# A separate pair of buffers for the last output group, and smaller first loads, in a fused attention + gMLP kernel

## Chip, cores, metric

The kernel runs on one core of one Trainium2 chip. The metric is device time in microseconds (us) of one execution, lower is better. Every quoted time is the median of several executions; a profile is of one execution, and its span (first to last instruction) is 1.7 to 1.9 us shorter than that execution's time. A run is called slow when it is over 1.5% above the fastest of its kernel; such runs are left out of the ratios, and where a median contains one, the table says so.

## Reference

A layer norm feeds a sliding-window attention (32 heads of 16, window 8, dilation 2) and a gated MLP with a spatial product. Both results are added to x. In short, with S = 2048 and D = 512 in bf16:

```python
xn = layernorm(x)                                  # [2048, 512]
q, k, v = split(xn @ wqkv)                         # wqkv [512, 1536]
attn = softmax(q . k at offsets 0,2,..,14) . v
z  = gelu(xn @ w_in)                               # [2048, 1376], halves z1, z2
g  = w_sp @ layernorm(z2) + b_sp                   # w_sp [2048, 2048]
out = x + attn @ wo + (z1 * g) @ w_out
```

## The kernel before

The work is planned by hand: every engine has a fixed order of instructions, TensorE is nearly always busy, and tiles of 128 tokens are grouped as four blocks j of four tiles tb. Only the two ends matter here.

**Start.** The first block's tiles ("x tiles 1 to 4") are loaded first: tiles 1 and 2 in halves on two issuing engines, tiles 3 and 4 in one transfer of 256 KB on ScalarE's queue. SyncE loads the query weights (512 KB, "first weights"), the second x block (512 KB) and the key weights (512 KB).

```python
def load_wqk(E, s):                                # s=0 query weights, s=1 key weights
    E.dma_start(wqk[:, s],
                A_wqkv[:, s * D:(s + 1) * D].rearrange("(k p) f -> p k f", p=P))

for tb in range(2):
    load_x0(SP, tb, 0)
    load_x0(A, tb, 1)
A.dma_start(xall[:, 0, 2:4, :], xblk[0][:, 2:4, :])
load_wqk(SP, 0)
SP.dma_start(xall[:, 1], xblk[1])
load_wqk(SP, 1)
for j in range(2, 4):
    SP.dma_start(xall[:, j], xblk[j])
SP.dma_start(w_z2[:], ...)
# ... cut: constants, layer norm helpers
pqs = [qk_tile() for _ in range(3)]
qk_part(pqs[0], 0, 0, 0, 2, kcs=range(2))          # query products of tiles 1, 2
qk_part(pqs[0], 0, 0, 0, 2, kcs=range(2, 4))
tr_copy(t0[2], tr(t0[2]))                          # transpose tile 3 on TensorE
qk_part(pqs[1], 0, 1, 0, 2, (0,))
tr_copy(t0[3], tr(t0[3]))                          # transpose tile 4
qk_part(pqs[1], 0, 1, 0, 2, (1,))
qk_part(pqs[0], 0, 0, 2, 3)                        # query products of tile 3: 16 matmuls of 128 columns
qk_part(pqs[1], 0, 1, 2, 3)
qk_part(pqs[2], 0, 2, 0, 2)                        # first key products: need the key weights
# ... cut
for n in range(2):
    qk_part(pqs[n], 0, n, 3, 4)                    # query products of tile 4
    qk_copy(pqs[n], 0, n)
```

VectorE takes each tile's statistics (`ln_stats`), ScalarE a square root, VectorE normalises the tile, TensorE transposes it. The statistics of tile 4 stand in VectorE's order ahead of tile 3's normalisation, so tile 3's transposition needs both tiles.

**End.** The output has four groups o of four tiles. Each tile's sum waits in PSUM; VectorE adds x to it (`out_add`) and SyncE or ScalarE stores the result. All four groups share four x buffers `xr_t` and four result buffers `ot_t`, which lie in the dead part of the q/k region:

```python
xr_t = [r_qk[:, QE + 4096 + n * D:QE + 4096 + (n + 1) * D] for n in range(4)]
ot_t = [r_qk[:, QE + 6144 + n * D:QE + 6144 + (n + 1) * D] for n in range(4)]

def load_xr(o):
    for tb in range(TB):
        i = 4 * tb + ORD[o]
        SP.dma_start(xr_t[tb], x2[i * P:(i + 1) * P, :])

def out_add(o, tb, part=0):
    pc, cs = tiles["o", o][tb][part]
    V.tensor_tensor(ot_t[tb][:, cs], pc, xr_t[tb][:, cs], ALU.add)

def out_store(o, tb, part=0, E=SP):
    i = 4 * tb + ORD[o]
    pc, cs = tiles["o", o][tb][part]
    E.dma_start(out2[i * P:(i + 1) * P, cs], ot_t[tb][:, cs])
```

So an addition of the last group may not overwrite a result buffer before the previous group's store from it has landed. `r_pr`, the region of the attention products, is free by then.

Of the kernel before, what the change touches and what calls it, by code (L numbers as in the profile page):

```python
# [11 lines left out]
ALU = mybir.AluOpType  # L12
# [3 lines left out]
P = 128  # L16
S = 2048
D = 512
NT = S // P
TB = 4  # L20
TBS = 512
C = D // P
# [48 lines left out]
def kernel(  # L71
# [13 lines left out]
    V = nc.vector  # L85
    A = nc.scalar
    G = nc.gpsimd
    PE = nc.tensor
    SP = nc.sync

    x2 = A_x.rearrange("b s d -> (b s) d")
    out2 = out.rearrange("b s d -> (b s) d")
    xblk = x2.rearrange("(b j p) d -> j p b d", b=TB, j=4)
# [9 lines left out]
    xall = r_x[:, 0:4 * TB * D].rearrange("p (j b d) -> p j b d", j=4, b=TB)  # L103
    vp = r_x[:].rearrange("p (d t) -> p d t", d=DH)
    r_w = sb.tile([P, 8192], BF16, name="r_w")
    wqk = r_w[:, 0:4096].rearrange("p (s k f) -> p s k f", s=2, k=C)
# [9 lines left out]
    xr_t = [r_qk[:, QE + 4096 + n * D:QE + 4096 + (n + 1) * D] for n in range(4)]  # L116
    ot_t = [r_qk[:, QE + 6144 + n * D:QE + 6144 + (n + 1) * D] for n in range(4)]
# [8 lines left out]
    r_pr = sb.tile([P, 2 * 4 * C * TB * P], BF16, name="r_pr")  # L126
# [2 lines left out]
    uT = r_uz[:, NZ1 * FPAD:].rearrange("p (s m t) -> p s m t", s=2, m=MCH)  # L129
    pr_home = [r_pr[:, 0:8192], r_pr[:, 8192:16384], r_uz[:, (NZ1 + 8) * FPAD - 8192:]]  # L130
    pr = [h.rearrange("p (c w b t) -> p c w b t", w=4, c=C, b=TB) for h in pr_home]
    pw_t = [r_pr[:, n * 2048:(n + 1) * 2048].rearrange("p (d t) -> p d t", d=DH) for n in range(4)]
    op = r_pr[:, 8192:16384].rearrange("p (d t) -> p d t", d=DH)

# [29 lines left out]
    def load_x0(E, tb, h):  # L164
        E.dma_start(xall[:, 0, tb, 256 * h:256 * h + 256], x2[tb * TBS:tb * TBS + P, 256 * h:256 * h + 256])  # L165

    def load_wqk(E, s):
        E.dma_start(wqk[:, s],
                    A_wqkv[:, s * D:(s + 1) * D].rearrange("(k p) f -> p k f", p=P))

    for tb in range(2):
        load_x0(SP, tb, 0)
        load_x0(A, tb, 1)
    A.dma_start(xall[:, 0, 2:4, :], xblk[0][:, 2:4, :])
    load_wqk(SP, 0)
    SP.dma_start(xall[:, 1], xblk[1])
    load_wqk(SP, 1)
    for j in range(2, 4):
        SP.dma_start(xall[:, j], xblk[j])
    SP.dma_start(w_z2[:], B_w_in[:, FH:F].rearrange("(k p) f -> p k f", p=P))  # L180
# [121 lines left out]
    def qk_part(pq, j, m, b0, b1, ccs=(0, 1), p0=None, kcs=range(C)):  # L302
        sd, c0 = m // 2, 2 * (m % 2)
        p0 = b0 if p0 is None else p0
        xv = xnT[:].rearrange("p k (b j t) -> p k b j t", b=TB, j=4)
        for cc in ccs:
            for kc in kcs:
                PE.matmul(pq[:, cc, p0 * P:(p0 + b1 - b0) * P], wqk[:, sd, kc, c0 + cc:D:C],  # L308
                          xv[:, kc, b0:b1, j, :], start=(kc == 0), stop=(kc == C - 1))

    def qk_copy(pq, j, m, b0=0, b1=TB, p0=None):
        sd, c0 = m // 2, 2 * (m % 2)
        p0 = b0 if p0 is None else p0
        if sd == 0:
            dst = qs[:, j, c0:c0 + 2, b0 * P:b1 * P].rearrange("p c (b t) -> p c b t", b=b1 - b0)
        else:
            dst = ks[:, c0:c0 + 2, HALO:HALO + S].rearrange("p c (b j t) -> p c b j t", b=TB, j=4)[:, :, b0:b1, j, :]
        cast = A.copy(dst, pq[:, :, p0 * P:(p0 + b1 - b0) * P].rearrange("p c (b t) -> p c b t", b=b1 - b0))  # L318
        if sd == 1:
            for i in k_reads[j]:  # L320
                tc.declare_no_dep(cast.ins, i, reason="other token columns of the same rows")
            k_casts[j].append(cast.ins)

    def qk_tile():
        return ps_mm.tile([P, 2, TBS], F32, name="pq", tag="mm")
# [147 lines left out]
    def load_xr(o):  # L473
        for tb in range(TB):
            i = 4 * tb + ORD[o]
            SP.dma_start(xr_t[tb], x2[i * P:(i + 1) * P, :])  # L476

    def out_heads(o):
        last = o == 3
# [30 lines left out]

    def out_add(o, tb, part=0):
        pc, cs = tiles["o", o][tb][part]
        V.tensor_tensor(ot_t[tb][:, cs], pc, xr_t[tb][:, cs], ALU.add)  # L513

    def out_store(o, tb, part=0, E=SP):
        i = 4 * tb + ORD[o]
        pc, cs = tiles["o", o][tb][part]
        E.dma_start(out2[i * P:(i + 1) * P, cs], ot_t[tb][:, cs])

    def out_full(o, tb, part=0):  # L520
        pc, cs = tiles["o", o][tb][part]
# [9 lines left out]
    def last_adds():  # L531
        for tb, part, E in ((2, 0, SP), (3, 0, A), (3, 1, SP)):
            out_add(3, tb, part)
            out_store(3, tb, part, E)
# [41 lines left out]
    pqs = [qk_tile() for _ in range(3)]  # L576
# [3 lines left out]
    qk_part(pqs[1], 0, 1, 0, 2, (0,))  # L580
    tr_copy(t0[3], tr(t0[3]))
    qk_part(pqs[1], 0, 1, 0, 2, (1,))
    qk_part(pqs[0], 0, 0, 2, 3)
    qk_part(pqs[1], 0, 1, 2, 3)
    qk_part(pqs[2], 0, 2, 0, 2)
    for n in range(2):
        ln_stats(i1[n])
# [4 lines left out]
    ln_apply(i1[1])  # L592
    ln_stats(i1[3])
    for n in range(2):
        qk_part(pqs[n], 0, n, 3, 4)
        qk_copy(pqs[n], 0, n)
    ln_sqrt(slice(9, 16, 4))
    ln_stats(i2[0])
# [22 lines left out]
    pqs = [qk_tile() for _ in range(3)]  # L621
# [32 lines left out]
    def halo_zero():  # L654
# [9 lines left out]
             "M": sm_max, "E": sm_exp, "S": lambda h, k: sm_sum(h, k), "R": sm_norm, "mask": add_mask,  # L664
             "G": g_mm, "Gi": g_bias, "U": u_mul, "T": u_tr, "A": lambda k: ap[k](),
             "O": out_heads, "Or": out_rest, "Oh": out_half, "F": out_add, "s": out_store, "end": last_adds,
             "halo": halo_zero, "wo": load_wo, "late": load_late, "xr": load_xr, "w": load_wsp}
    for tok in ORDER.split():
        name = tok.rstrip("0123456789.")
# [31 lines left out]
```

## Time and profile before

| | before |
|---|---|
| time, median of 3 runs | 203.91 us (203.90 to 204.33) |
| the profiled execution | 204.95 us, span 203.2 us |
| TensorE busy | 97% of the span |
| start: VectorE waits for x tiles 3 and 4 | 0.87 us |
| end: last addition starts after TensorE's end | 0.66 us |

From the page of the profile before: its head, the busy times, and the chain of waits that ended last, as shares of the span.

```profile
span 203.2 us, 4070 instructions
PE 196.3 (97%) x1687; PEld 124.8 (61%) x1691; DVE 187.2 (92%) x267; ACT 100.1 (49%) x162; POOL 11.2 (6%) x14
...
PE 89%; DMA 4%; DVE 2%; SPq 2%; issue 1%; ACTq 0%; DVEq 0%
```

PE is TensorE, PEld its weight loads, DVE VectorE, ACT ScalarE, SPq and ACTq the issuing of transfers. The chain is TensorE but for some microseconds, and those lie at the ends.

The timeline of before at the start. Columns: start in us, duration, engine, line, operation, output<-input, shapes, count, and in brackets the idle time ahead of it and what ended it.

```profile
1.72 0.43 SPq L168 DMA_DIRECT2D r_w<-in_A_wqkv_dram  x1
1.73 0.46 ACTq L174 DMA_DIRECT2D r_x<-in_A_x_dram  x1
...
2.19 0.51 SPq L176 DMA_DIRECT2D r_x<-in_A_x_dram  x1
...
2.74 0.51 SPq L168 DMA_DIRECT2D r_w<-in_A_wqkv_dram  x1
...
5.57 0.41 DVE L216 TENSOR_SCALAR r_x<-r_x,mv,rstd 128x512 bf16<-128x512 bf16 x1
...
6.85 0.69 DVE L205 BATCH_NORM_STATS2 stats<-r_x 128x6 f32<-128x512 bf16 x1 [0.87 <-DMA r_x<-in_A_x_dram]
...
9.11 0.40 PE L223 MATMUL pt<-ident,r_x 128*128 128x128 bf16 x4 [1.18 <-DVE r_x L216]
```

VectorE has tile 2 normalised at 5.98 and then waits 0.87 us for tile 3, whose load was issued at 1.73. TensorE pays for it at 9.11, with the transposition of tile 3. The other lines are the issues of the first weights (1.72), the second x block (2.19) and the key weights (2.74).

The timeline of before at the end:

```profile
196.52 4.62 SPq L518 DMA_DIRECT2D out_dram<-r_qk  x6
...
197.61 0.69 DVE L513 TENSOR_TENSOR r_qk<-po,r_qk 128x512 bf16<-128x512 f32 x1 [5.02 <-PE po L523]
198.83 0.69 DVE L513 TENSOR_TENSOR r_qk<-po,r_qk 128x512 bf16<-128x512 f32 x1 [0.53 <-DMA out_dram<-r_qk]
199.10 0.64 PE L523 MATMUL pb<-r_w,r_uz 128*128 128x224 bf16 x5
199.44 1.05 DVE L513 TENSOR_TENSOR r_qk<-pa,r_qk 128x512 bf16<-128x512 f32 x2
200.40 0.38 DVE L513 TENSOR_TENSOR r_qk<-pb,r_qk 128x224 bf16<-128x224 f32 x1
```

The second addition waits 0.53 us for a store (the previous group's, from the same result buffer). TensorE ends at 199.10 + 0.64 = 199.74, and the last addition begins only at 200.40.

### The profile page before, as it was taken

How to read it: one execution, taken by the hardware profiler on the slowest of the kernel's cores; microseconds unless marked ns; L12 is line 12 of the kernel's file. 1: busy time of each engine (PE TensorE's matmuls, PEld its weight loads, DVE VectorE, ACT ScalarE, POOL GpSimd, SP SyncE). 2: the span in 40 equal slices, each digit the busy share in tenths (PEclk: the TensorE clock that was granted, in tenths of full speed). 3: DMA queues.
4: the chain of work that ended last, by engine and by line, in shares of the span. 5: the costliest groups of instructions: out<-in, count | busy, mean ns of one | idle time of the engine just before them, and what ended most of it. 6: DMA issues, size and time to landing. Idle time of an engine off the chain costs nothing.

```text
span 203.2 us, 4070 instructions
## 1 busy us (share of the span) xinstructions
PE 196.3 (97%) x1687; PEld 124.8 (61%) x1691; DVE 187.2 (92%) x267; ACT 100.1 (49%) x162; POOL 11.2 (6%) x14
## 2 busy tenths in 40 slices
PE   7699999999999999999999999999999999999993
PEld 2499866565566666666556666666546645664561
DVE  5789899999999999999989998999999999999714
ACT  3566999999969984641742309546100210131000
POOL 3000000592000000000000000000000000000000
PEclk9999999999999999999999999999999999999999
DMA  4972548200298000695699957997927910743253
GB/s 151 357 253 53 101 99 177 76 0 3 55 185 176 3 0 0 120 257 113 29 212 198 215 155 103 209 175 148 194 40 196 222 26 14 212 110 93 51 185 130
DMA packets 66290, 25.91 MB, mean 127 GB/s; under 512 B 56224, under 2 KB 66016, under 8 KB 66016
## 3 DMA queue, kind: packets, MB, share of 16 engines
q1 hardware_dynamic: 65568, 25.19, 54.7%
q10 hardware_dynamic: 704, 0.47, 0.7%
q8 instruction: 13, 0.21, 0.5%
q14 instruction: 5, 0.04, 0.1%
HBM read 10.13 MB, written 2.10 MB: 60 GB/s over the span
## 4 chain that ended last, share of the span: by engine, by line
PE 89%; DMA 4%; DVE 2%; SPq 2%; issue 1%; ACTq 0%; DVEq 0%
PE pg L451 37%; PE pz L237 18%; PE pq L308 13%; PE pv L412 7%; PE po L523 6%; PE po L499 5%; DMA r_x<-in_A_x_dram 3%; SPq L476 1%; DVE r_qk L513 1%; PE pl L362 1%; DMA out_dram<-r_qk 1%; PE po L508 1%; DVE stats L205 1%; PE pt L223 1%; ACTq L165 0%
## 5 line engine op out<-in xcount | busy, mean ns | idle before, releaser
L451 PE MATMUL pg<-z,r_qk 128*128 128x344 bf16 x448 | 67.3, 309 | 0.0
L451 PEld LDWEIGHTS <-r_qk 128*128 128x128 bf16 x448 | 43.7, 98 | 22.4 <-issue 0.8
L237 PE MATMUL pz<-w_z,xnT 128*128 128x344 bf16 x256 | 40.1, 309 | 0.0
L426 DVE TENSOR_TENSOR r_pr<-r_x,r_w 128x2048 bf16<-128x2048 bf16 x32 | 38.2, 1217 | 0.3
L430 DVE TENSOR_TENSOR r_pr<-r_pr 128x2048 bf16<-128x2048 bf16 x28 | 33.8, 1217 | 0.2
L457 ACT ACTIVATE gs<-pg,b_col 128x688 bf16<-128x688 f32 x16 | 13.3, 832 | 40.6 <-PE pg L451 25.1
L237 PEld LDWEIGHTS <-xnT 128*128 128x128 bf16 x256 | 24.9, 98 | 13.4 <-issue 0.8
L308 PE MATMUL pq<-xnT,r_w 128*128 128x256 bf16 (+2 forms) x192 | 28.7, 303 | 0.1
L342 DVE TENSOR_TENSOR r_pr<-r_qk 128x2048 bf16<-128x2048 bf16 x24 | 28.4, 1216 | 0.0
L308 PEld LDWEIGHTS <-r_w 128*128 128x128 bf16 x200 | 20.3, 114 | 7.1 <-DMA r_w<-in_A_wqkv_dram 0.4
L299 ACT ACTIVATE r_uz<-pz 128x688 bf16<-128x688 f32 x16 | 11.5, 742 | 22.5 <-PE pz L237 22.3
L318 ACT CAST r_qk<-pq 128x1024 bf16<-128x1024 f32 (+1 forms) x16 | 15.3, 990 | 2.4 <-PE pq L308 2.3
L523 PE MATMUL po<-r_w,r_uz 128*128 128x512 bf16 x66 | 14.9, 379 | 0.6 <-issue 0.6
L513 DVE TENSOR_TENSOR r_qk<-po,r_qk 128x512 bf16<-128x512 f32 x14 | 9.2, 684 | 6.5 <-PE po L523 6.0
L412 PE MATMUL pv<-xnT,r_w 128*32 128x512 bf16 x256 | 14.6, 380 | 0.0
L499 PE MATMUL po<-r_lg,r_pr 32*128 32x512 bf16 x224 | 14.5, 375 | 0.0
L523 PEld LDWEIGHTS <-r_uz 128*128 128x128 bf16 x85 | 8.0, 98 | 9.7 <-issue 1.5
L351 DVE TENSOR_TENSOR r_pr<-r_pr 128x4096 bf16<-128x4096 bf16 x6 | 13.7, 2281 | 0.0
L205 DVE BATCH_NORM_STATS2 stats<-r_x 128x6 f32<-128x512 bf16 (+1 forms) x18 | 10.9, 615 | 2.1 <-DMA r_x<-in_A_x_dram 2.1
L261 ACT ACTIVATE junk<-z 128x688 bf16<-128x688 bf16 x16 | 12.5, 778 | 0.2
L412 PEld LDWEIGHTS <-r_w 128*32 128x32 bf16 x256 | 9.5, 138 | 4.5 <-issue 0.3
L255 ACT ACTIVATE z<-pz 128x688 bf16<-128x688 f32 x16 | 11.8, 739 | 0.8 <-PE pz L237 0.8
(81 smaller groups left out, 174.6 us busy)
## 6 DMA issues: line engine op xcount, KB each, us to landing
r_lg<-in_A_wo_dram SPq DMA_DIRECT2D x8, 256.0 KB, 4.2
r_qk<-in_A_x_dram SPq DMA_DIRECT2D x16, 128.0 KB, 2.4
out_dram<-r_qk SPq DMA_DIRECT2D x15, 128.0 KB, 2.1
r_w<-in_A_wqkv_dram SPq DMA_DIRECT2D x3, 512.0 KB, 5.2
r_x<-in_A_x_dram SPq DMA_DIRECT2D x3, 512.0 KB, 6.0
w_z<-in_B_w_in_dram SPq DMA_DIRECT2D x2, 688.0 KB, 5.6
r_w<-in_B_w_out_dram SPq DMA_DIRECT2D x1, 640.0 KB, 5.0
r_x<-in_A_x_dram ACTq DMA_DIRECT2D x1, 256.0 KB, 5.1
```

The lines of the kernel that those rows point to most:

```text
L237: PE.matmul(pz[:, hh, 0:FHALF], xnT[:, kc, i * P:(i + 1) * P], wz[:, kc, hh * FHALF:(hh + 1) * FHALF], start=(kc == 0), stop=(kc == C - 1))
L308: PE.matmul(pq[:, cc, p0 * P:(p0 + b1 - b0) * P], wqk[:, sd, kc, c0 + cc:D:C], xv[:, kc, b0:b1, j, :], start=(kc == 0), stop=(kc == C - 1))
L318: cast = A.copy(dst, pq[:, :, p0 * P:(p0 + b1 - b0) * P].rearrange("p c (b t) -> p c b t", b=b1 - b0))
L342: prod = V.tensor_tensor(pr[g % 3][:, c].rearrange("p w b t -> p b w t"), q3.unsqueeze(2).broadcast_to([P, TB, 4, P]), k4, ALU.mult)
L351: V.tensor_tensor(pr[g % 3][:, 0:2], pr[g % 3][:, 0:2], pr[g % 3][:, 2:4], ALU.add)
L412: PE.matmul(pv[32 * tb:32 * tb + 32, dd, :], wv[:, kc, 2 * d2 + dd, :], xnT[:, kc, tb * TBS:(tb + 1) * TBS], start=(kc == 0), stop=(kc == ...
L426: V.tensor_tensor(pw_t[n], vp[:, :, off:off + P], a_sb[:, slot_w(w), ts].unsqueeze(1).broadcast_to([P, DH, P]), ALU.mult)
L430: V.tensor_tensor(pw_t[n] if dst is None else dst, pw_t[n], pw_t[m], ALU.add)
L451: PE.matmul(pg[:, hh, 0:FHALF], wsp[n][:, k, :], z2[:, k, hh * FHALF:(hh + 1) * FHALF], start=(k == 0), stop=(k == NT - 1))
L457: A.activation(gs[:], tiles.pop(("g", n))[:, :, 0:FHALF], ACT.Identity, bias=b_col[:, i:i + 1])
L499: PE.matmul(pc, op[32 * tb:32 * tb + 32, d, o * P:(o + 1) * P], wo_r[32 * tb:32 * tb + 32, d, cs], start=(d == 8), stop=False, tile_positi ...
L523: PE.matmul(pc, uT[:, o % 2, m, tb * P:(tb + 1) * P], wout[:, m, cs], start=False, stop=(m == MCH - 3))
```

## The change

Its intent has two parts. At the end, the last group gets its own x and result buffers in the free products' region, so that no addition waits for a store. At the start, x tiles 3 and 4, the first weights and the second x block each come in two transfers, so that the first halves land sooner; the key weights go ahead of the second half of the x block; and the query products of tiles 3 and 4 are computed together in matmuls of 256 columns, which also moves tile 3's behind the first key products. The order in which the rest of the kernel's steps are queued is the same. This is the whole diff:

```diff
--- before.py
+++ after.py
@@ -129,6 +129,8 @@
     uT = r_uz[:, NZ1 * FPAD:].rearrange("p (s m t) -> p s m t", s=2, m=MCH)
     pr_home = [r_pr[:, 0:8192], r_pr[:, 8192:16384], r_uz[:, (NZ1 + 8) * FPAD - 8192:]]
     pr = [h.rearrange("p (c w b t) -> p c w b t", w=4, c=C, b=TB) for h in pr_home]
+    xl_t = [r_pr[:, n * D:(n + 1) * D] for n in range(4)]
+    ol_t = [r_pr[:, (4 + n) * D:(5 + n) * D] for n in range(4)]
     pw_t = [r_pr[:, n * 2048:(n + 1) * 2048].rearrange("p (d t) -> p d t", d=DH) for n in range(4)]
     op = r_pr[:, 8192:16384].rearrange("p (d t) -> p d t", d=DH)
 
@@ -164,17 +166,20 @@
     def load_x0(E, tb, h):
         E.dma_start(xall[:, 0, tb, 256 * h:256 * h + 256], x2[tb * TBS:tb * TBS + P, 256 * h:256 * h + 256])
 
-    def load_wqk(E, s):
-        E.dma_start(wqk[:, s],
-                    A_wqkv[:, s * D:(s + 1) * D].rearrange("(k p) f -> p k f", p=P))
+    def load_wqk(E, s, k0=0, k1=C):
+        E.dma_start(wqk[:, s, k0:k1],
+                    A_wqkv[:, s * D:(s + 1) * D].rearrange("(k p) f -> p k f", p=P)[:, k0:k1])
 
     for tb in range(2):
         load_x0(SP, tb, 0)
         load_x0(A, tb, 1)
-    A.dma_start(xall[:, 0, 2:4, :], xblk[0][:, 2:4, :])
-    load_wqk(SP, 0)
-    SP.dma_start(xall[:, 1], xblk[1])
+    for tb in range(2, TB):
+        A.dma_start(xall[:, 0, tb], xblk[0][:, tb])
+    load_wqk(SP, 0, 0, 2)
+    load_wqk(SP, 0, 2, 4)
+    SP.dma_start(xall[:, 1, 0:2], xblk[1][:, 0:2])
     load_wqk(SP, 1)
+    SP.dma_start(xall[:, 1, 2:4], xblk[1][:, 2:4])
     for j in range(2, 4):
         SP.dma_start(xall[:, j], xblk[j])
     SP.dma_start(w_z2[:], B_w_in[:, FH:F].rearrange("(k p) f -> p k f", p=P))
@@ -473,7 +478,7 @@
     def load_xr(o):
         for tb in range(TB):
             i = 4 * tb + ORD[o]
-            SP.dma_start(xr_t[tb], x2[i * P:(i + 1) * P, :])
+            SP.dma_start((xl_t if o == 3 else xr_t)[tb], x2[i * P:(i + 1) * P, :])
 
     def out_heads(o):
         last = o == 3
@@ -510,12 +515,13 @@
 
     def out_add(o, tb, part=0):
         pc, cs = tiles["o", o][tb][part]
-        V.tensor_tensor(ot_t[tb][:, cs], pc, xr_t[tb][:, cs], ALU.add)
+        xr, ot = (xl_t, ol_t) if o == 3 else (xr_t, ot_t)
+        V.tensor_tensor(ot[tb][:, cs], pc, xr[tb][:, cs], ALU.add)
 
     def out_store(o, tb, part=0, E=SP):
         i = 4 * tb + ORD[o]
         pc, cs = tiles["o", o][tb][part]
-        E.dma_start(out2[i * P:(i + 1) * P, cs], ot_t[tb][:, cs])
+        E.dma_start(out2[i * P:(i + 1) * P, cs], (ol_t if o == 3 else ot_t)[tb][:, cs])
 
     def out_full(o, tb, part=0):
         pc, cs = tiles["o", o][tb][part]
@@ -580,8 +586,6 @@
     qk_part(pqs[1], 0, 1, 0, 2, (0,))
     tr_copy(t0[3], tr(t0[3]))
     qk_part(pqs[1], 0, 1, 0, 2, (1,))
-    qk_part(pqs[0], 0, 0, 2, 3)
-    qk_part(pqs[1], 0, 1, 2, 3)
     qk_part(pqs[2], 0, 2, 0, 2)
     for n in range(2):
         ln_stats(i1[n])
@@ -592,7 +596,7 @@
     ln_apply(i1[1])
     ln_stats(i1[3])
     for n in range(2):
-        qk_part(pqs[n], 0, n, 3, 4)
+        qk_part(pqs[n], 0, n, 2, 4)
         qk_copy(pqs[n], 0, n)
     ln_sqrt(slice(9, 16, 4))
     ln_stats(i2[0])
```

## Prediction

> **What bounds the kernel now.** The chain of waits is 89% TensorE, and the table of waits shows TensorE waiting only at the two ends; between 9.11 us and 199.7 us it has no gap above 0.2 us. VectorE is busy 92%, but nothing there waits for it. So only start and end can give time.
>
> *Start.* The timeline shows VectorE free at 5.98 us (second tile normalised) and starting the third tile's statistics at 6.85: 0.87 us of waiting for the 256 KB load of x tiles 3 and 4 (landed 5.1 us after issue). The rest follows at a fixed distance: root, normalisation 8.64, transposition 9.11, before which TensorE idled 1.18 us. The first weight matrix (512 KB) landed at the same time. From 4 us the DMA engines run full at about 360 GB/s. The Trainium skill ("DMA: Bandwidth & Descriptors", section "Issuing engines are not separate DMA queues") says that queues interleave on the same 16 engines; the common landing at 6.8 us agrees.
>
> *End.* TensorE ends at 199.74. VectorE's last additions should follow it, but the second starts at 198.83, 0.53 us after the first ended, "released by DMA out": it overwrites a result buffer whose store was issued at 196.52 and landed at 198.75. The third (199.44) waits likewise. The last addition starts at 200.40, 0.66 us behind TensorE.
>
> **What the change does.**
> 1. x tiles 3 and 4 come as two 128 KB transfers, the weights as two 256 KB ones. My estimate, from cumulated GB/s of the windows (768 KB of both queues landed at 6.75; half of it is moved about 1 us earlier): tile 3 and the first weight half land at 5.4 to 5.9, before VectorE is free; tile 4 at 6.2 to 6.8, needed at 6.8. Gain: the full 0.87 us, at most 0.3 less; all engines shift together.
> 2. The key weights go ahead of half of the second x block: landed (estimate) at about 9, needed at about 9.6, as TensorE reaches them 1.7 us earlier. In the compiled program each transfer waits for the eighth before it, so later loads are issued 0.5 to 1 us later; a backlog of 768 KB hides that.
> 3. 32 matmuls of 128 columns (56 ns each in the chain) become 16 of 256 (109 ns): nothing.
> 4. The last group reads x and writes results in the products' buffers, free since 188.7. Queue order there is unchanged; x lands at 196.8 to 198.5, early enough. Additions start at 197.61, 198.22, 198.83, 199.44, 199.80 (spacing from the trace): 0.60 us gained, all on the chain to the last store.
>
> Sum: 0.85 + 0.6 = 1.45 us; I take off 0.05: **202.5 us, 202.1 to 203.3** eight times in ten. Faster by over 2%: 1%; within 2%: 98%; slower: 1%.
>
> **What would show it.** Right: third tile's statistics at about 6.0 and its transposition at about 8.25; TensorE idle before it 0.3 us; no gap later; last addition within 0.15 us of the last matmul; no wait for a store in the last group. Wrong: statistics still waiting for x after 6.3; TensorE waiting for key weights near 9.6; an addition waiting for x; TensorE gaps later that give the gain back.
>
> **What would make it wrong.** Smaller transfers landing no earlier, since the engines drain everything together (203.3); late key weights; the first x load of the last group, whose issue took 1.57 us, arriving late (up to 0.5 us). A gain above 1.5 us I see no source for.

## Result and the profile after

A ratio here is the mean time of one kernel's fast runs over the mean of the other's of the same rounds, so it is not quite the ratio of the medians.

| | before | after | ratio, 95% interval |
|---|---|---|---|
| median of 4 runs each, same chip | 204.12 (203.9 to 204.7) | 203.77 (203.56 to 203.85) | 0.9977 (0.9953 to 1.0001) |
| profiled execution: time | 204.95 | 203.85 | |
| profiled execution: span | 203.2 | 202.0 | |

Within 2%, as was held likely; but the predicted 1.4 us became 0.35 in the medians, outside the range of 202.1 to 203.3. The two profiles differ by 1.2 us, nearly what was predicted. Profiles and times do not tell the same story, and that is the first thing to explain.

The page of after: head, busy times, chain.

```profile
span 202.0 us, 4038 instructions
PE 196.5 (97%) x1671; PEld 124.7 (62%) x1675; DVE 187.1 (93%) x267; ACT 100.0 (50%) x162; POOL 11.5 (6%) x14
...
PE 90%; DMA 3%; DVE 2%; SPq 2%; ACTq 1%; issue 1%; DVEq 0%
```

Timeline of after, start:

```profile
1.72 0.95 SPq L170 DMA_DIRECT2D r_w<-in_A_wqkv_dram  x2
1.73 0.96 ACTq L177 DMA_DIRECT2D r_x<-in_A_x_dram  x2
...
3.14 0.37 SPq L180 DMA_DIRECT2D r_x<-in_A_x_dram  x1
...
3.55 0.47 SPq L170 DMA_DIRECT2D r_w<-in_A_wqkv_dram  x1
...
5.71 0.68 DVE L210 BATCH_NORM_STATS2 stats<-r_x 128x6 f32<-128x512 bf16 x1
...
6.79 0.69 DVE L210 BATCH_NORM_STATS2 stats<-r_x 128x6 f32<-128x512 bf16 x1 [0.18 <-DMA r_x<-in_A_x_dram]
...
8.26 0.40 PE L228 MATMUL pt<-ident,r_x 128*128 128x128 bf16 x4 [0.51 <-DVE r_x L221]
...
9.74 2.98 PEld L313 LDWEIGHTS <-r_w 128*128 128x128 bf16 x28 [0.26 <-DMA r_w<-in_A_wqkv_dram]
```

Tile 3 no longer makes VectorE wait, tile 4 by 0.18 us, and TensorE transposes tile 3 at 8.26 instead of 9.11. But the key weights are issued at 3.55 instead of 2.74, and TensorE's weight loads wait for them at 9.74, which they did not before.

Timeline of after, end:

```profile
196.91 1.29 DVE L519 TENSOR_TENSOR r_pr<-po,r_pr 128x512 bf16<-128x512 f32 x2 [5.02 <-PE po L529]
...
198.11 1.04 DVE L519 TENSOR_TENSOR r_pr<-pa,r_pr 128x512 bf16<-128x512 f32 x2
198.40 0.64 PE L529 MATMUL pb<-r_w,r_uz 128*128 128x224 bf16 x5
199.08 0.39 DVE L519 TENSOR_TENSOR r_pr<-pb,r_pr 128x224 bf16<-128x224 f32 x1
```

No addition waits for a store. The last one begins 0.04 us after TensorE's end at 199.04.

### The profile page after: what moved, and what is told of

It reads as the page before. It is cut to its first block, busy times and chain, and to the rows that moved or that the text cites. A ratio compares the mean times of both kernels' runs of the same rounds, so it can differ in the third digit from the quotient of the medians.

```text
span 202.0 us, 4038 instructions
## 1 busy us (share of the span) xinstructions
PE 196.5 (97%) x1671; PEld 124.7 (62%) x1675; DVE 187.1 (93%) x267; ACT 100.0 (50%) x162; POOL 11.5 (6%) x14
## 4 chain that ended last, share of the span: by engine, by line
PE 90%; DMA 3%; DVE 2%; SPq 2%; ACTq 1%; issue 1%; DVEq 0%
PE pg L456 37%; PE pz L242 19%; PE pq L313 13%; PE pv L417 7%; PE po L529 6%; PE po L504 5%; DMA r_x<-in_A_x_dram 2%; SPq L481 1%; PE pl L367 1%; DMA r_pr<-in_A_x_dram 1%; DVE r_pr L519 1%; PE po L513 1%; DVE r_qk L519 1%; PE pt L228 1%; ACTq L167 0%
## 5 line engine op out<-in xcount | busy, mean ns | idle before, releaser
L313 PE MATMUL pq<-xnT,r_w 128*128 128x256 bf16 (+1 forms) x176 | 28.9, 316 | 0.1
L304 ACT ACTIVATE r_uz<-pz 128x688 bf16<-128x688 f32 x16 | 11.5, 742 | 22.5 <-PE pz L242 22.1
L504 PEld LDWEIGHTS <-r_pr 32*128 32x128 bf16 x272 | 7.6, 93 | 6.5 <-issue 0.6
```

Source lines behind the costliest of these rows:

```text
L313: PE.matmul(pq[:, cc, p0 * P:(p0 + b1 - b0) * P], wqk[:, sd, kc, c0 + cc:D:C], xv[:, kc, b0:b1, j, :], start=(kc == 0), stop=(kc == C - 1))
L504: PE.matmul(pc, op[32 * tb:32 * tb + 32, d, o * P:(o + 1) * P], wo_r[32 * tb:32 * tb + 32, d, cs], start=(d == 8), stop=False, tile_positi ...
```

## Experiments

The expectations call the theories by letters:

- **A**: the profile predicted from was of an unusually long execution, so part of the predicted gain was never there. **B**, its rival: time and span are offset differently in the two kernels.
- **Q**: before has two kinds of execution, according to which of two issues comes first at 1.7 us: ScalarE's load of x tiles 3 and 4, or SyncE's load of the first weights.
- **R**: the regrouped matmuls removed 0.9 us of other work (16 matmuls of 56 ns) that had covered the key weights' landing.
- **S**: smaller transfers themselves make later loads late. **L**, its rival: what counts is that loads are *issued* late, because each transfer waits in the compiled program for the eighth before it, and two more transfers move the second x block and the keys behind a first x load (in after, the x block's first half goes out at 3.14, 0.02 us after the first of the x loads has landed at 3.12).

### 1. Both kernels again, and each part alone

Short edits: the first and the last are the kernels before and after, unchanged. Tail only is before with

```diff
-            SP.dma_start(xr_t[tb], x2[i * P:(i + 1) * P, :])
+            SP.dma_start((xl_t if o == 3 else xr_t)[tb], x2[i * P:(i + 1) * P, :])
 # and ol_t for ot_t where o == 3, in out_add and out_store
```

and start only is after with those lines undone.

Before again: 

> The unchanged kernel against itself. Theory A (the profile I predicted from was an execution about 1 us slower than the usual one: 204.95 us against a median of 203.91): the spans of these runs are mostly 202.0 to 202.5 us, about 1.75 us below the times, and the new profile lacks one of the two waits (start 0.87 us, or end 0.6 us). Theory B (the span is usually 203.2 us and the time has another, smaller part outside the span): spans near 203.2 us with times near 204.0. Ratio 1.000 +- 0.001 in both.

Tail only: 

> Only the last group's own buffers. If the wait at the end is in every run: 0.5 to 0.6 us faster than before (ratio 0.997). If that wait was an accident of the one profile (theory A, end): 0 to 0.15 us (ratio 0.9993 to 1.000).

Start only: 

> Only the smaller first loads and the regrouped matmuls. If the wait for the x tiles at the start is in every run: 0.7 us faster (ratio 0.9966; the trace after showed 0.70). If it was an accident of the one profile (theory A, start): 0 to 0.3 us.

After again: 

> The whole change. Theory A: 0.3 to 0.5 us faster (ratio 0.998), spans 201.8 to 202.0. If the parts add: the sum of the two single parts within 0.15 us. Theory B: same ratio, but spans 1.2 us below those of the unchanged kernel.

| run | median | ratio to before, 95% | profiled execution: time, span |
|---|---|---|---|
| before again | 203.95 | 1.0003 (0.9979 to 1.0027) | 203.83, 202.1 |
| tail only | 203.40 | 0.9978 (0.9955 to 1.0001) | 204.07, 202.3 |
| start only | 205.27 (205.02 without the slow run) | 1.0057 (1.0023 to 1.0091) | 207.83, 206.1 (slow, clock 0.992) |
| after again | 204.24 | 1.0010 (0.9981 to 1.0039) | 204.09, 202.4 |

Time minus span is 1.7 to 1.9 us in every run: B falls. A holds: before's second profile is of an execution close to the median of its series, and it looks different. It is called the usual one below, but with care: in the later series before's medians were 204.00 to 204.60, and its 55 runs in the comparison show no gap between two groups of times. So executions without the wait exist; how frequent they are in before is not shown. Chain of waits on its page, and its timeline:

```profile
PE 94%; DVE 3%; DMA 1%; DVEq 0%; issue 0%
```

```profile
1.71 0.46 ACTq L174 DMA_DIRECT2D r_x<-in_A_x_dram  x1
...
1.75 0.43 SPq L168 DMA_DIRECT2D r_w<-in_A_wqkv_dram  x1
...
5.89 0.69 DVE L205 BATCH_NORM_STATS2 stats<-r_x 128x6 f32<-128x512 bf16 x1
...
8.17 0.40 PE L223 MATMUL pt<-ident,r_x 128*128 128x128 bf16 x4
...
197.72 0.69 DVE L513 TENSOR_TENSOR r_qk<-po,r_qk 128x512 bf16<-128x512 f32 x1 [0.35 <-DMA out_dram<-r_qk]
...
198.16 0.64 PE L523 MATMUL pb<-r_w,r_uz 128*128 128x224 bf16 x5
...
199.29 0.38 DVE L513 TENSOR_TENSOR r_qk<-pb,r_qk 128x224 bf16<-128x224 f32 x1
```

There is no wait for x at all. The same kernel transposes tile 3 at 8.17 and not at 9.11, and DMA falls from 4% of the chain to 1%. The wait at the end is there, a little smaller: the last addition begins 0.49 us after TensorE's end (198.80).

Tail only gains about what it should. Start only *loses*, and in its one profile TensorE stands for the key weights (the execution was slow, but at 11.5 us the wait is a landing, not a clock):

```profile
11.51 0.74 PE L313 MATMUL pq<-xnT,r_w 128*128 128x256 bf16 x5 [1.92 <-DMA r_w<-in_A_wqkv_dram]
```

So the start part of the change costs something, and in this trace what it costs has to do with the keys. The two parts do not add within the 0.15 us that was expected: their ratios come to +0.35% together, and after again has +0.10%, though the intervals allow for such a difference. Start only is the one variant whose interval lies wholly above 1, and its only trace is of the slow run; why it loses more than after does stays open.

### 2. Is it the regrouping, the splits, or the queue order?

Four kernels, all with the new tail. "Split, old matmuls" is after with the 16 matmuls put back ahead of the key products:

```diff
+    qk_part(pqs[0], 0, 0, 2, 3)
+    qk_part(pqs[1], 0, 1, 2, 3)
     qk_part(pqs[2], 0, 2, 0, 2)
...
-        qk_part(pqs[n], 0, n, 2, 4)
+        qk_part(pqs[n], 0, n, 3, 4)
```

"Regrouped" is the tail with only the reverse of that edit. "x first" moves the load of tiles 3 and 4 to SyncE's queue, ahead of the first weights. The fourth repeats the tail.

```diff
-    A.dma_start(xall[:, 0, 2:4, :], xblk[0][:, 2:4, :])
+    SP.dma_start(xall[:, 0, 2:4, :], xblk[0][:, 2:4, :])
     load_wqk(SP, 0)
```

Split, old matmuls: 

> The whole change with the matmul regrouping undone (32 products of 128 columns again, half of them ahead of the key products). Theory R (the regrouping took away 0.9 us of matmuls that stood between the transposition of tile 4 and the first use of the key weights, so TensorE now waits for them): no wait for weights before the key products or under 0.1 us, and about 0.5 us faster than the whole change was (203.4 to 203.6 us). Theory S (the smaller transfers themselves make the loads land late and unevenly on the 16 engines): still slower than the last-group change alone by 0.5 us or more (203.9 to 204.8), keys landing at 9.7 or later, the last of 16 parts over 0.6 us behind the middle one.

Regrouped: 

> Last group's buffers and the regrouping, with the old large loads. Keys landed at 9.40 and 9.69 us in the two traces of the unchanged kernel. Theory R: TensorE waits for the keys by 0.2 to 0.6 us in an execution where x landed early, 0.1 or less in one where x landed late; time 0.2 to 0.4 us above the last-group change alone. Theory S: as fast as the last-group change alone (within 0.15 us).

x first: 

> Last group's buffers, old loads, but x tiles 3 and 4 stand on SyncE's queue ahead of the weights instead of on ScalarE's beside them. Theory Q (two modes of the unchanged kernel: whether ScalarE or SyncE is first by some 10 ns decides whether x lands at 5.1 or 6.8 us): only the fast mode is left, no wait of VectorE for tile 3, spread of the runs under 0.4 us, median 203.2 to 203.4. Rival (the modes have another origin): two groups of times 0.7 us apart remain.

Tail again: 

> The last-group change alone once more, as the base of these three: 0.5 us faster than before; by theory Q two groups of times, near 203.3 and 204.1 us.

| run | median | ratio to before, 95% |
|---|---|---|
| tail + split, old matmuls | 203.95 | 0.9984 (0.9958 to 1.0010) |
| tail + regrouped | 203.97 | 0.9985 (0.9961 to 1.0008) |
| tail + x first | 203.67 | 0.9996 (0.9953 to 1.0038), one run of 206.25 in it |
| tail again | 203.67 | 0.9969 (0.9944 to 0.9994) |

R alone does not explain it: with the old order put back, TensorE in that profile still waits 0.67 us for the keys, which landed at 11.43. The times of this round are too close to rank the variants. The traces say more, and they are set out together after the last experiment. For Q the third kernel is ambiguous: its x landed early (4.62) and its profiled run took 203.32, but its median is above the 203.2 to 203.4 that was expected, its runs spread by more than 0.4 us even without the one of 206.25 (whose clock was 0.992), and its interval is wide.

### 3. One split at a time, and a late issue without a split

The first three have the tail and one of the three splits each (tiles 3 and 4; first weights; second x block with the keys in between). The fourth has no split, but two tiny loads of 8 KB ahead of the second x block, so that the block and the keys are issued as late as in after:

```diff
+    pad = sb.tile([P, 2, 256], BF16, name="pad")
+    for n in range(2):
+        SP.dma_start(pad[0:16, n, :], x2[16 * n:16 * n + 16, 0:256])
     SP.dma_start(xall[:, 1], xblk[1])
     load_wqk(SP, 1)
```

Tiles 3 and 4 split: 

> Last group's buffers plus only the first of the three splits: x tiles 3 and 4 in two transfers on ScalarE's queue. Gap between the middle and the last of the 16 parts of the key weights' landing: with the old loads 0.2 to 0.7 us in six traces, with all splits 0.8 to 2.4 us in four. Theory L (what hurts is that later loads are issued late, as each waits for the eighth before it): only the key weights wait for a first load here, gap under 0.7 and key landing 9.4 to 9.9 us; time within 0.2 us of the last-group change alone, and less spread. Rival S1 (this split is the guilty one): gap over 0.8 us, time 0.3 to 0.6 us higher.

First weights split: 

> Last group's buffers plus only the second split: the first weight matrix in two transfers. Theory L: as the last-group change alone within 0.2 us, gap under 0.7. Rival S2 (this split is guilty): gap over 0.8 us and keys after 9.9 us, time 0.3 to 0.6 us higher.

Second x block split: 

> Last group's buffers plus only the third split: second x block in two halves with the key weights between them. By bytes the keys should land 0.7 us earlier, near 8.8 us, and the second half of x near 9.6, gap under 0.7 (theory L: nothing is issued late here). Rival S3: gap over 0.8 us, keys not before 9.4.

Late issue: 

> Last group's buffers, the old large loads, but two loads of 8 KB that nothing reads stand ahead of the second x block on SyncE's queue, so that it and all later loads wait for the first x loads and are issued about 1 us later (x block at 3.1 to 3.3 us instead of 2.2). Theory L: the same picture as with the splits: long packets after 5.5 us, gap over 0.8 us, time 0.3 us or more above the last-group change alone. Rival (small transfers are guilty, not the time of issue): gap under 0.7, time within 0.2 us.

| run | median | ratio to before, 95% |
|---|---|---|
| tail + tiles 3, 4 split | 203.83 | 0.9992 (0.9975 to 1.0010) |
| tail + first weights split | 203.82 | 0.9989 (0.9975 to 1.0002) |
| tail + second x block split | 203.43 | 0.9981 (0.9960 to 1.0003) |
| tail + late issue, no split | 204.05 (203.95 without the slow run) | 1.0007 (0.9987 to 1.0026) |

With the late issue alone, and large loads throughout, the tail's gain is gone: that speaks for L, though the tail alone was not run on this chip. Its profile fell in a slow execution (348.33 us, clock 0.56), so only the loads at the start are read from it; the median of its five fast runs is 203.95, against 204.0 for before on the same chip. In the timeline of that run, the key weights (line L170, the second time) go out at 3.77, not at 2.74. They landed at 10.41, which is 1.94 us after tile 3's transposition, and TensorE did not wait for them (at this clock it also comes to them later). So this trace shows a late landing, but not where the five fast runs lost their time:

```profile
1.73 0.46 ACTq L176 DMA_DIRECT2D r_x<-in_A_x_dram  x1
1.76 0.45 SPq L170 DMA_DIRECT2D r_w<-in_A_wqkv_dram  x1
2.25 1.01 SPq L180 DMA_DIRECT2D pad<-in_A_x_dram  x2
...
3.30 0.42 SPq L181 DMA_DIRECT2D r_x<-in_A_x_dram  x1
3.77 0.51 SPq L170 DMA_DIRECT2D r_w<-in_A_wqkv_dram  x1
```

The third split adds one transfer but leaves the key weights' issue at 2.83, and the keys land at 8.81, earlier than in before. So a split by itself does no harm: S falls as a general rule. The split of the first weights, however, came out as its rival S2 had it and not as L did: a gap of 1.02 us, and keys at 10.43. There the additional issue alone moves the second x block from 2.2 to 2.73, so L (only the wait for the eighth load before) is too narrow; that the time of issue decides is a reading made after this run. The split of tiles 3 and 4 was expected to be within 0.2 us of the tail alone, and was not (203.83); its profile shows why in that execution (the second tile's last part landed only at 4.53), but not why in the median. That stays open. (Its expectation names gaps of 0.8 to 2.4 us for four traces with all splits; start only's is 2.74.)

### 4. The race at 1.7 us

The next four: an attempt to win the race by issuing tiles 3 and 4 at 1.24 us, one issue earlier; the third split again; the same with the regrouping; and after once more.

```diff
-    for tb in range(2):
-        load_x0(SP, tb, 0)
-        load_x0(A, tb, 1)
+    load_x0(SP, 0, 0)
+    load_x0(A, 0, 1)
+    SP.dma_start(xall[:, 0, 1], xblk[0][:, 1])
     A.dma_start(xall[:, 0, 2:4, :], xblk[0][:, 2:4, :])
```

Tail, third split, earlier x: 

> Last group's buffers, third split (keys between the halves of the second x block), and the load of x tiles 3 and 4 moved up on ScalarE's queue (issued at about 1.24 us; SyncE takes the whole second tile), so that it is ahead of the first weights (1.72) by half a microsecond in every execution. Theory Q: tiles 3 and 4 land by 5.2 us, VectorE never waits for them, the runs lie within 0.4 us of each other, median 203.1 to 203.4. Rival (the modes have another origin): two groups of times 0.7 us apart again, or the second tile now lands too late (after 4.2 us) and the gain is lost.

Tail, third split again: 

> Last group's buffers and third split, once more. Theory L: second x block issued at 2.2 us, keys land at 8.6 to 9.0 with a gap under 0.7 us; 0.4 to 0.6 us faster than before.

The same, regrouped: 

> The same plus the regrouped matmuls, that is the whole change without its first two splits. If the regrouping costs only because the keys are late: no wait for the keys (they land near 8.8, wanted from 9.3 on), time within 0.15 us of the one without regrouping.

After again: 

> The whole change on the same chip as the three above. Theory L: second x block issued after 3.0 us, gap over 0.7, key landing 9.7 or later, TensorE waits for keys 0.2 us or more; 203.7 to 204.3 us, 0.3 to 0.7 us behind the version with the third split alone.

| run | median | ratio to before, 95% |
|---|---|---|
| earlier x | 204.33 | 1.0005 (0.9980 to 1.0030) |
| third split again | 203.39 | 0.9967 (0.9942 to 0.9992) |
| third split, regrouped | 203.77 | 0.9974 (0.9950 to 0.9998) |
| after again | 204.09 | 0.9993 (0.9969 to 1.0018) |

The first attempt failed as a test: tiles 3 and 4 landed early (4.94), but now tile 2, a single transfer, landed late, and VectorE waited there instead. From its timeline (the second line of statistics is tile 2):

```profile
4.78 0.75 DVE L208 BATCH_NORM_STATS2 stats<-r_x 128x6 f32<-128x256 bf16 x2 [0.68 <-DMA r_x<-in_A_x_dram]
```

After again shows a start as good as before's, and the loss at the keys in full. Its timeline:

```profile
3.68 0.47 SPq L170 DMA_DIRECT2D r_w<-in_A_wqkv_dram  x1
...
8.17 0.40 PE L228 MATMUL pt<-ident,r_x 128*128 128x128 bf16 x4
...
10.22 2.05 PE L313 MATMUL pq<-xnT,r_w 128*128 128x256 bf16 x17 [0.56 <-DMA r_w<-in_A_wqkv_dram]
...
13.30 0.39 PE L228 MATMUL pt<-ident,r_x 128*128 128x128 bf16 x4
...
198.87 0.64 PE L529 MATMUL pb<-r_w,r_uz 128*128 128x224 bf16 x5
```

Both this kernel and before in its usual execution transpose tile 3 at 8.17. Before then reaches its last group of matmuls at 198.16, after at 198.87. Nothing later gives the 0.7 us back. The third split, regrouped, has no wait for the keys in its trace, as expected; but its median is 0.38 us above that without the regrouping (by the ratios 0.14 us), where 0.15 us had been allowed, and the intervals are too wide to decide between them.

### 5. The race decided

The last two make SyncE's weight load wait for something short, so that ScalarE's x load is always first. VectorE's clearing of constants moves ahead of the loads, and one column of the weight buffer is cleared last of them; the weights may only be loaded after it. The result stays right, since the load overwrites that column.

```diff
+    V.memset(warm[:, 0:P], 0.0)
+    V.memset(eps_t[:], EPS)
+    V.memset(ks[:, :, 0:HALO], 0.0)
+    V.memset(z1u[:, 0:NZ1 - 1, FH:FPAD], 0.0)
+    V.memset(wqk[:, 0, 0, 0:1], 0.0)
     for tb in range(2):
         load_x0(SP, tb, 0)
 # the first four memsets are removed where they stood
```

Tail, third split, gate: 

> Last group's buffers, third split, and the first weights held back until a clearing of one of their columns by VectorE, which ends at about 1.85 us, so that ScalarE's load of x tiles 3 and 4 (issued 1.71 to 1.74) is ahead of them in every execution by 0.1 to 0.2 us, with nothing else moved. Theory Q: tiles 3 and 4 land by 5.6 us, no wait of VectorE for tile 3, no group of times 0.7 us higher: all runs 203.2 to 203.6, a late first load excepted; 0.5 to 0.9 us faster than before. Rival (the modes have another origin): two of six runs at 203.9 or above, as without the gate.

Tail, gate: 

> Last group's buffers and the same gate, old loads. Theory Q: as above; 203.2 to 203.6 in all runs. If the third split is worth something by itself, this is slower than the one with it by 0.1 us or more; with keys landing near 9.4 us and wanted at about 10.3 I expect no difference.

| run | median | all six runs | ratio to before, 95% |
|---|---|---|---|
| tail + third split + gate | 203.53 | 203.04 to 203.83 | 0.9954 (0.9932 to 0.9976) |
| tail + gate | 203.46 | 203.16 to 203.65 | 0.9946 (0.9926 to 0.9966) |

Before's eleven runs run beside them lie between 203.86 and 205.30. Timeline of tail + gate: the weights go out at 1.85, 0.14 us behind x and right after the clearing of one column.

```profile
1.71 0.46 ACTq L181 DMA_DIRECT2D r_x<-in_A_x_dram  x1
1.77 0.06 DVE L177 MEMSET r_w<- 128x1 bf16 x1
...
1.85 0.39 SPq L170 DMA_DIRECT2D r_w<-in_A_wqkv_dram  x1
...
5.91 0.69 DVE L208 BATCH_NORM_STATS2 stats<-r_x 128x6 f32<-128x512 bf16 x1
...
8.20 0.40 PE L226 MATMUL pt<-ident,r_x 128*128 128x128 bf16 x4
```

This version, the tail of the change, none of its start, and one ordering, beats before clear of noise. The size is less certain: before took 204.60 in this series and 203.91 in the first one on this chip, so the 0.9 to 1.1 us in the ratios are more than that series would give. After was not run beside it; 203.46 is 0.3 to 0.8 us below after's three medians. Five of the twelve gated runs lie outside the 203.2 to 203.6 that was expected, by at most 0.23 us, and there is no group 0.7 us higher. With the race decided the third split adds nothing, as expected.

**The race, from all traces.** For the kernels that load tiles 3 and 4 whole on ScalarE and the first weights whole on SyncE, and whose first x loads are as in before (the trace records when each part of a transfer lands):

| x issued ahead of the weights by | traces | x tiles 3 and 4 land |
|---|---|---|
| 29 to 143 ns | before again, tail regrouped, tail + third split, late issue, both gated | 5.08 to 5.75 us |
| -13 to +6 ns | before, tail (twice), third split again, the same regrouped | 6.49 to 6.94 us |

No trace lies between 6 and 29 ns. In the first gated trace x goes out at 1.737, as in the second row, and still lands at 5.60, because the weights go out at 1.856: so it is the order that counts, not the time of x. The packets agree: by 4.0 us ScalarE's queue had moved 224 to 288 KB of its 384 in the traces of the first row, and 129 to 153 KB, little more than the halves of tiles 1 and 2, in those of the second. In the 24 runs of the two ungated kernels (tail, and tail + third split, in two series each) 16 took 203.20 to 203.48 us and 8 took 203.95 to 204.58, none between; the four profiled among them fall in the group that their landing says, and the granted clock was 0.998 or more in all 24, so it does not make the groups. With the gate all 12 runs lie at 203.83 or below. So Q is shown: a difference of some tens of nanoseconds in issue moves the landing by 0.7 us or more, and about a third of the runs of these two kernels have the late kind. The gate removes it.

**Where the time is, trace by trace.** In each trace not marked slow, three numbers are read from the timeline: when tile 3's transposition starts (T), when TensorE's last matmuls start (L), and how far the last addition follows TensorE's end.

| trace | T | keys issued | keys landed | L - T | last addition behind |
|---|---|---|---|---|---|
| before | 9.11 | 2.74 | 9.69 | 189.99 | 0.66 |
| before again | 8.17 | 2.82 | 9.40 | 189.99 | 0.49 |
| tail, two traces | 8.77, 8.77 | 2.75, 2.76 | 9.74, 9.69 | 189.99, 189.99 | 0.04 |
| tail + tiles 3, 4 split | 8.71 | 2.90 | 9.60 | 190.00 | 0.04 |
| tail + first weights split | 8.34 | 3.25 | 10.43 | 189.99 | 0.04 |
| tail + x first | 7.91 | 3.27 | 9.78 | 190.00 | 0.04 |
| tail + third split, two traces | 8.16, 9.23 | 2.83, 2.77 | 8.81, 9.53 | 190.00, 189.99 | 0.04 |
| the same, earlier x | 8.94 | 2.82 | 8.79 | 189.99 | 0.04 |
| tail + third split + gate | 7.88 | 2.85 | 8.86 | 190.00 | 0.04 |
| tail + gate | 8.20 | 2.84 | 9.64 | 190.00 | 0.04 |
| tail + third split, regrouped | 8.83 | 2.75 | 8.99 | 189.96 | 0.04 |
| tail + regrouped | 8.48 | 2.82 | 10.05 | **190.27** | 0.04 |
| after, three traces | 8.26, 8.36, 8.17 | 3.55, 3.44, 3.68 | 9.70, 10.02, 10.17 | **190.14, 190.36, 190.70** | 0.04 |
| tail + split, old matmuls | 8.43 | 3.65 | 11.43 | **191.01** | 0.04 |

The whole middle of the kernel takes 190.00 us within 0.01 in every trace with the old matmul order, except the one whose keys landed at 11.43. So, up to the start of the last addition, the difference between two traces is the sum of three terms and nothing else: the start T, the loss in L - T, and the tail. From there to the end of the span, the last store included, it took 2.76 to 3.02 us, which the table leaves out.

The loss follows one rule in the regrouped order. The keys landed 1.44, 1.66, 2.00 us (after) and 1.57 us (tail + regrouped) behind T, and the losses against 190.00 are 0.14, 0.36, 0.70 and 0.27: in each of the four, landing minus loss is T + 1.30. That is when the regrouped order wants the keys. In the old order 2.09 us behind T still cost nothing (tail + first weights split). So with the old matmul order, keys that landed as they did in after would have been in time; and with keys as early as in the third split, the regrouped order loses nothing (8.99, which is T + 0.16). The loss in after needs both: the late landing and the earlier need. Only where keys land 3.00 us behind T, as in split, old matmuls, does the landing alone suffice. There the loss of 1.01 us is more than TensorE's wait of 0.67; VectorE also waits 1.10 us for the second x block in that trace, and how the rest divides was not tested.

**Why keys land late.** A load raises its semaphore in 16 steps, one for each DMA engine. The Trainium skill ("DMA: Bandwidth & Descriptors", section "Why a DMA increments its semaphore by 16 and not by 1") says that the engines finish independently and only the full 16 means that all has landed. The traces agree, 16 updates for each of the loads at the start. Where the second x block was issued by 2.29 us (12 traces), the last part of the key load came 0.16 to 0.76 us after the middle one; where it was issued at 2.71 us or later (8 traces), 0.62 to 2.74 us. The two groups overlap from 0.62 to 0.76 us. The late-issue kernel is among the latter (0.88, keys at 10.41) without any split. So the late issue, and not the splits as such, is the likely cause; one trace, of a slow execution, does not show it beyond doubt.

The packets show one step more. Between 6.0 and 7.5 us the DMA engines moved 361 to 376 GB/s in the traces with the early issue (290 in the one with the earlier x), but 237 to 269 in the five with all three splits and 312 to 340 in the other three with a late issue. In the five, the engines' busy share fell to 0.56 to 0.75 in the worst half microsecond: they were partly without work, so what was queued behind landed later. *Why* one of sixteen parts then falls behind the others is not shown, and stays open.

## Why the prediction was wrong

**"Gain: the full 0.87 us, at most 0.3 less": this step failed.** The wait was real, but by the traces it belongs to one of two kinds of execution. The profile was of an execution of 204.95 us in a kernel whose median is 203.91, and this stood in the results beside the profile. Before in its usual execution (203.83 us) starts tile 3's statistics at 5.89 without a wait and transposes at 8.17; after's three traces have 8.26, 8.36 and 8.17. So against such an execution this term is 0 and not 0.85. Only in executions in which x loses the race do the splits give something (9.11 and 8.77 in traces of the old loads).

**"The key weights go ahead of half of the second x block: landed (estimate) at about 9, needed at about 9.6": this step failed too.** They landed at 9.70, 10.02 and 10.17 in the three traces of after, and were wanted at T + 1.30, which is 9.56, 9.66 and 9.47. Going ahead of half a block in the queue is worth less than an issue that is 0.6 to 0.9 us later. "A backlog of 768 KB hides that" was the error: the late issue was seen, and dismissed. The backlog did not keep the DMA engines full: in these three traces they moved 237 to 269 GB/s between 6.0 and 7.5 us, against 361 and 372 in the two traces of before. The loss is 0.14, 0.36 and 0.70 us in L - T, and all of it stays to the end.

**"32 matmuls of 128 columns become 16 of 256: nothing": right as a duration, incomplete as a step.** With the keys early (8.99), the regrouped kernel has an L - T of 189.96, so 0.04 us gained. But the 16 matmuls that moved had stood ahead of the key products, 16 x 56 ns = 0.9 us of cover. Regrouped, TensorE wants the keys at T + 1.30; in the old order at T + 2.2 by an estimate from before's usual trace (9.06 + 0.44 + 0.9 = 10.4, less T = 8.17; in that trace the first key product starts at 10.39), and T + 2.09 was shown to be in time. So R is a real part of the cause, and the late landing is the other.

**"0.60 us gained" at the end: right.** The last addition follows TensorE by 0.04 us in every trace with the new buffers, against 0.49 and 0.66 before: 0.45 to 0.62 us. The times of the tail alone agree: ratios 0.9978 and 0.9969, which is 0.45 and 0.63 us of 204. No addition waits for x, and x's slow first issue was no problem.

**"Smaller transfers landing no earlier" and "late key weights" as dangers:** the second came true, and was put at a size that the range did not hold.

**The sum.** Predicted: 0.85 + 0.60 - 0.05 = 1.40 us. Measured in three series of runs, after stands at 0.9977, 1.0010 and 0.9993 of before, on average 0.14 us faster, and the tail alone about 0.54 us faster. So the start part costs about 0.4 us on average, where 0.85 us had been predicted as a gain; start only, measured by itself, cost 1.2 us (0.5 to 1.9). In the terms of the table, the last of after's traces (8.17, 190.70, 0.04) against before in its usual execution (8.17, 189.99, 0.49) is +0.71 - 0.45 = +0.26 us, and after's other two come to +0.11 and -0.21 in the same way; against before in the late execution (9.11, 189.99, 0.66) the three are -0.85, -1.00 and -1.32 us. The mean lies between, presumably according to how often x loses the race; after's own runs spread from 203.53 to 205.10 us in one series, so its three traces do not cover all that it does. (With the last store in them, the spans of the three differ from before again's by +0.4, +0.3 and -0.1 us.) The two profiles set side by side after the change, at -1.2 us, compared a bad execution of one kernel with a good one of the other.

What stays open: why a late issue makes one part of a transfer fall behind; why the split of tiles 3 and 4 alone gained nothing in the median; why start only loses most; and what moves the first x loads by some tenths of a us between executions.

## What to carry to other kernels

Before predicting from a wait, compare the profiled execution's own time with the median; if it is longer, the wait may be what makes it longer, and a second profile of the unchanged kernel is the cheapest experiment there is. Where a wait for a load comes and goes, look for two queues that issue within some tens of nanoseconds of each other, and decide the order yourself rather than cut the transfers. Cutting them into more pieces has a price in the issue times of the loads behind them, and work moved away from in front of a load's first use takes away its cover even when its own duration is unchanged.

## What the Trainium skill lacked or had wrong

- "DMA: Bandwidth & Descriptors", section "Issuing engines are not separate DMA queues", says that transfers issued by different engines run on the same 16 DMA engines and interleave, and that issuing on several engines only saves issue time. It does not say that the order in which two queues start can decide by much when the smaller one lands: with x issued 29 to 143 ns ahead, its 256 KB landed at 5.08 to 5.75 us; with the two within 13 ns, at 6.49 to 6.94 us.
- The same page, section "Why a DMA increments its semaphore by 16 and not by 1", tells that the 16 parts finish independently, which the traces confirm, but gives no idea of how far apart: here 0.16 to 0.76 us between the middle and the last part for key loads behind an early issue, and 0.62 to 2.74 us behind a late one.
- "Perfetto Trace Analysis" has no warning that a trace shows one execution, which may not be a typical one: here the first profile of before had a span of 203.2 us and a wait for x of 0.87 us, and the next one of the same kernel 202.1 us and no such wait.
